# Who issues the second half of the first token tile: SyncE's queue or ScalarE

## The chip, the cores and the metric

The kernel runs on one core of one Trainium2 chip. The time is device microseconds of that core, the median of several runs. A profile is a single execution of the program, recorded by the hardware profiler; its span goes from the first to the last instruction of the core.

## The reference

The computation is a gated mix of two branches over one sequence `x` of 2048 tokens with 448 channels, all in float32:

```
g = sigmoid((x * gate_w).sum(-1))
q, k, v = split(x @ wqkv)                        # 16 heads of 28
a = (softmax over 8 keys, 2 tokens apart) @ wo   # sliding, dilated attention
b = relu(x @ w1 + b1)**2 @ w2 + b2               # 1792 hidden units
out = g * a + (1 - g) * b
```

## The kernel before

TensorE (PE in the profile) does all the large products. To keep nearly float32 accuracy, each operand is split into a high part (rounded to the matmul's type) and a low part (the rest), and each product is three matmuls: high by high, high by low, low by high. ScalarE (ACT) rounds to the high part, VectorE (DVE) subtracts it from the raw data to get the low part. GpSimd (POOL) does the products of the attention, which is too narrow for TensorE.

The tokens are cut into four chunks of 512; the 448 channels, over which the products sum, into three row tiles of 128 channels (k = 0, 1, 2) and one of 64 (k = 3), which is stored twice so that two 64-row matmuls can run side by side. The phases follow each other on TensorE: q, k and v of the chunks, then both layers of the MLP, with the output projection of the attention fitted in between. The order of all work is written out by hand; a counter of estimated TensorE time decides while the program is built where a piece of another engine's work is put.

The change is in the start. L629 to L634 clear a tile `zero` on VectorE and run 13 filler matmuls (`WARM`) on TensorE that need no input. From L637 on the first inputs are fetched: `raws[0]` (`wqraw` in the profile), the weights of q, and `rx` (`xraw`), the tokens of chunk 0 with channels on the partitions. The loop over k issues the weights of row tile k (L641, for k = 3 L644) and then its tokens (L646). For k = 0 the tokens come in two transfers of 256 tokens each (128 KB), for the others in one (256 KB). Behind them, on the same queue, come the weights of k and v (L651, L654) and the tokens of chunk 1 (L565). All of these are issued by SyncE (SP), one after another; 224 transfers of the program go that way, and no other engine issues any.

The splits follow at L656: for each k ScalarE rounds the weights (L657) and the two halves of the tokens (L664), except the very first half, which VectorE rounds (L662). ScalarE's first instruction is a table load that belongs to the first of these (L657). VectorE makes the low parts (L665, L667).

TensorE's first real matmuls are those of `qkv_first` (L255). It works on four blocks of 128 tokens, and for each k it does the pair of blocks 0 and 1 and then 2 and 3, six matmuls each: twice high by high, twice the weights' low part, twice the tokens' low part. The first six of a k need its weights and the first half of its tokens, the other six the second half as well. The thirteenth is the first of k = 1. Then come the matmuls with 64 rows (L186) for k = 3 and all later products.

A transfer that reuses a completion semaphore first waits for the earlier transfer on it. There are eight of these in turn, so from the ninth transfer on SyncE waits, before it issues, for an earlier one to have landed.

Of the kernel before, what the change touches and what calls it, by code (L numbers as in the profile page):

```python
# [22 lines left out]
CH = 512  # L23
# [34 lines left out]
def gated_mix_kernel(ctx: ExitStack, tc: tile.TileContext, xT, wqkv, w1, w2, wo, b1, b2, out):  # L58
    nc = tc.nc
# [437 lines left out]
    def raw_tile(name):  # L497
        return rawp.tile([P, 4, 512], F32, tag="raw", name=name)
# [139 lines left out]
    rx = raw_tile("xraw0")  # L638
    for k in range(4):
        if k < 3:  # L640
            nc.sync.dma_start(raws[0][:, k, :NQ], wqkv[0, :, k])  # L641
        else:
            for b, rows in ((0, slice(0, 64)), (1, slice(64, P))):
                nc.sync.dma_start(raws[0][rows, k, :NQ], wqkv[b, rows, k])  # L644
        for cols in ((slice(0, 256), slice(256, CH)) if k == 0 else (slice(0, CH),)):
            nc.sync.dma_start(rx[:, k, cols], xT[0, :, k, cols])  # L646

    for b, tag in ((1, "k"), (2, "v")):
        raw = attp.tile([P, 3, D], F32, tag=tag, name=f"wqraw{b}")
# [571 lines left out]
```

## Time and profile before

| | |
|---|---|
| Time, median of 3 runs | 413.23 us (413.23 to 413.26) |
| The profiled execution's own time | 413.8 us |
| Its span | 412.0 us |
| Granted TensorE clock, mean | 1.000 |
| DMA, whole span | 73.83 MB, mean 179 GB/s |
| Idle of ScalarE up to 12 us, by DMA of tokens | 2.8 us in 3 waits, longest 1.6 |
| Idle of ScalarE up to 12 us, by DMA of weights | 1.6 us in 2 waits, longest 1.4 |

A row of the timeline has the start and the duration in us, the engine, the line, the operation, what it writes and reads, the shapes and a count, and in brackets the idle time of the engine before it with what ended it. Neighbouring instructions that are alike stand in one row, so a duration can be that of several. `PEld` is TensorE's weight loader, which works ahead of the matmuls. `SPq` rows are the time that SyncE takes to issue a transfer, not the transfer itself. A table by stretch of time has, for each engine, the busy time and the count of instructions, and last the clock, the busy share of the 16 DMA engines and what they moved.

### The profile page before, as it was taken

How to read it: one execution, taken by the hardware profiler on the slowest of the kernel's cores; microseconds unless marked ns; L12 is line 12 of the kernel's file. 1: busy time of each engine (PE TensorE's matmuls, PEld its weight loads, DVE VectorE, ACT ScalarE, POOL GpSimd, SP SyncE). 2: the span in 40 equal slices, each digit the busy share in tenths (PEclk: the TensorE clock that was granted, in tenths of full speed). 3: DMA queues.
4: the chain of work that ended last, by engine and by line, in shares of the span. 5: the costliest groups of instructions: out<-in, count | busy, mean ns of one | idle time of the engine just before them, and what ended most of it. 6: DMA issues, size and time to landing. Idle time of an engine off the chain costs nothing.

```text
span 412.0 us, 9331 instructions
## 1 busy us (share of the span) xinstructions
PE 407.8 (99%) x3835; PEld 366.0 (89%) x3835; DVE 270.6 (66%) x430; ACT 210.4 (51%) x461; POOL 268.4 (65%) x167
## 2 busy tenths in 40 slices
PE   8999999999999999999999999999999999999997
PEld 7999999999888888888888888989898888888996
DVE  4590745276767766787656798879576677892354
ACT  4641646387775555444565535444653254346540
POOL 0000001955999999989989899999899977940000
PEclk9999999999999999999999999999999999999999
DMA  7999999979262315654112649765146530168304
GB/s 213 368 351 309 286 390 288 355 223 315 91 241 99 128 51 209 208 186 152 41 47 105 222 158 270 196 146 154 28 157 200 217 130 2 45 179 132 95 0 181
DMA packets 66763, 73.83 MB, mean 179 GB/s; under 512 B 33120, under 2 KB 59296, under 8 KB 66464
## 3 DMA queue, kind: packets, MB, share of 16 engines
q1 hardware_dynamic: 66720, 73.23, 55.4%
q8 instruction: 30, 0.49, 0.5%
q14 instruction: 13, 0.11, 0.1%
HBM read 45.74 MB, written 28.28 MB: 180 GB/s over the span
## 4 chain that ended last, share of the span: by engine, by line
PE 99%; DVE 0%; issue 0%
PE b L186 33%; PE h L186 32%; PE qkv L186 23%; PE a L186 7%; PE qkv L255 2%; PE warm L634 1%; PE a L993 1%; PE last L993 0%; DVE bt L872 0%; PE last L985 0%; PE a L985 0%; DVE zero L631 0%; DVE b1z L632 0%
## 5 line engine op out<-in xcount | busy, mean ns | idle before, releaser
L335 POOL TENSOR_TENSOR qk<-q,k 128x896 f32<-128x896 f32 x64 | 135.2, 2144 | 84.2 <-DMA k<-k_d 76.0
L342 POOL TENSOR_TENSOR av<-lg,v 128x896 f32<-128x896 f32 x64 | 119.2, 1957 | 6.2 <-DVE lg L336 5.6
L621 DVE TENSOR_TENSOR h<-h,h 128x512 fp32r<-128x512 f32 x56 | 38.4, 688 | 66.8 <-ACT h L624 66.5
L186 PE MATMUL qkv<-wqh,x 64*128 64x448 f32 x528 | 78.2, 359 | 0.0
L336 DVE TENSOR_REDUCE lg<-qk 128x32 f32<-128x896 f32 x64 | 67.0, 1074 | 0.0
L350 DVE TENSOR_REDUCE o<-av 128x112 f32<-128x896 f32 x64 | 66.4, 1070 | 0.1
L186 PE MATMUL b<-w2ah,h 64*128 64x448 f32 x448 | 66.3, 359 | 0.0
L186 PE MATMUL b<-w2bh,h 64*128 64x448 f32 x448 | 66.1, 359 | 0.0
L622 ACT ACTIVATE h<-h,b1z 128x512 f32<-128x512 f32 x56 | 36.7, 655 | 43.6 <-PE h L186 43.6
L186 PEld LDWEIGHTS qkv<-wqh,x 64*128 64x128 f32 x528 | 49.4, 184 | 3.6
L186 PE MATMUL qkv<-wql,x 64*128 64x448 f32 x264 | 47.7, 358 | 0.0
L186 PEld LDWEIGHTS b<-w2bh,h 64*128 64x128 f32 x448 | 42.1, 184 | 3.5
L186 PEld LDWEIGHTS b<-w2ah,h 64*128 64x128 f32 x448 | 42.0, 184 | 3.7
L205 ACT ACTIVATE st<-qkv 128x448 f32<-128x448 f32 x48 | 23.5, 542 | 34.3 <-PE qkv L186 31.7
L186 PE MATMUL b<-w2bl,h 64*128 64x448 f32 x224 | 40.7, 358 | 0.0
L186 PE MATMUL b<-w2al,h 64*128 64x448 f32 x224 | 40.5, 358 | 0.0
L623 ACT ACTIVATE h<-h 128x512 fp32r<-128x512 f32 x56 | 33.5, 598 | 1.7
L624 ACT ACTIVATE h<-h 128x512 f32<-128x512 f32 x56 | 33.3, 594 | 0.0
L573 ACT ACTIVATE h<-h 128x4 fp32r<-128x4 f32 (+1 forms) x35 | 7.2, 207 | 44.4 <-PE b L186 44.2
L186 PE MATMUL h<-x2b,w1h 64*128 64x512 f32 x168 | 28.1, 386 | 0.0
L186 PE MATMUL h<-x,w1h 64*128 64x512 f32 x168 | 28.1, 386 | 0.0
L186 PE MATMUL h<-x1b,w1h 64*128 64x512 f32 x168 | 28.1, 386 | 0.0
(150 smaller groups left out, 688.6 us busy)
## 6 DMA issues: line engine op xcount, KB each, us to landing
k<-k_d SPq DMA_DIRECT2D x8, 840.0 KB, 5.6
v<-v_d SPq DMA_DIRECT2D x8, 840.0 KB, 5.0
x_d<-x SPq DMA_DIRECT2D x11, 512.0 KB, 6.8
q_d<-st SPq DMA_DIRECT2D x8, 448.0 KB, 5.5
k_d<-st SPq DMA_DIRECT2D x8, 448.0 KB, 5.2
v_d<-st SPq DMA_DIRECT2D x8, 448.0 KB, 5.8
w1raw<-w SPq DMA_DIRECT2D x4, 896.0 KB, 9.2
q<-q_d SPq DMA_DIRECT2D x8, 448.0 KB, 3.6
```

The lines of the kernel that those rows point to most:

```text
L186: nc.tensor.matmul(acc.pt[:, :acc.n], a[rows], w[rows], start=acc.todo == acc.all, stop=acc.todo == 1)
L205: nc.scalar.activation(st[:, :, t % 2], pt[:, :D].rearrange("p (g c) -> p g c", g=G), AF.Copy)
L255: nc.tensor.matmul(acc.pt[:, :D], a, w, start=k == j == 0, stop=False)
L335: nc.gpsimd.tensor_mul(pr, q[:, s:s + 1].to_broadcast([P, W, C]), k[:, s:s + W])
L336: pending.append(lambda: nc.vector.tensor_reduce(lg[:, s], pr.rearrange("p w (h d) -> p w h d", h=HG), axis=AX.X, op=ALU.add))
L342: nc.gpsimd.tensor_mul(pr.rearrange("p (h d) w -> p w h d", h=HG), lg[:, s][:, :, :, None].to_broadcast([P, W, HG, DH]), v[:, s:s + W].rea ...
L350: nc.vector.tensor_reduce(o[:, g * C:(g + 1) * C], pr, axis=AX.X, op=ALU.add)
L573: nc.scalar.activation(ap, f32(ap), AF.Copy)
L621: nc.vector.tensor_sub(hl, pt, f32(hh))
L622: ops += [lambda pt=pt, r=r: nc.scalar.activation(pt, pt, AF.Relu, bias=b1t[:, f + r:f + r + 1]), lambda pt=pt, hh=hh: nc.scalar.activatio ...
L623: lambda pt=pt, hh=hh: nc.scalar.activation(hh, pt, AF.Square),
L624: lambda pt=pt, r=r, low=low: (nc.scalar.activation(pt, pt, AF.Square), at(delays[r], low))]
```

## The change

The tokens 256 to 511 of row tile k = 0 are issued by ScalarE's queue (`nc.scalar`) instead of SyncE's, and in the program's order before the first half. In the order of ScalarE's instructions the issue is the first one, ahead of the table load of L657 and the first weight split. On SyncE's queue one transfer is missing; the others keep their order. What is moved, where to, and all computation stay the same. From here on the profile of the changed kernel has line numbers that are up to 3 higher.

```diff
-        for cols in ((slice(0, 256), slice(256, CH)) if k == 0 else (slice(0, CH),)):
-            nc.sync.dma_start(rx[:, k, cols], xT[0, :, k, cols])
+        if k == 0:
+            nc.scalar.dma_start(rx[:, 0, 256:CH], xT[0, :, 0, 256:CH])
+            nc.sync.dma_start(rx[:, 0, 0:256], xT[0, :, 0, 0:256])
+        else:
+            nc.sync.dma_start(rx[:, k], xT[0, :, k])
```

The completion semaphores are dealt out in the program's order: the first and the second half of these tokens swap theirs, so the tokens of k = 3, issued later by SyncE, wait for the landing of ScalarE's transfer before they are issued, where before they waited for the first half.

## The prediction

> **What bounds the kernel now.** I read the page first: its span, its busy times and the chain of work that ended last.
>
> ```profile
> span 412.0 us, 9331 instructions
> PE 407.8 (99%) x3835; PEld 366.0 (89%) x3835; DVE 270.6 (66%) x430; ACT 210.4 (51%) x461; POOL 268.4 (65%) x167
> ...
> PE 99%; DVE 0%; issue 0%
> ```
>
> TensorE (PE) is busy for 407.8 of 412.0 us and the chain is PE for 99%. So the change can pay only where PE stands still or runs slowly, and everything behind such a place moves by what is won or lost there. The waits of the weight loader (PEld) over the whole span say where PE stands still (total, times, longest):
>
> ```profile
> PEld warm L634 <- DVE b1z L632: 1.2, 1, 1.2
> PEld a L993 <- issue: 0.3, 1, 0.3
> PEld qkv L186 <- ACT wqh L115: 0.3, 1, 0.3
> PEld qkv L255 <- ACT x L664: 0.3, 1, 0.3
> PEld qkv L255 <- ACT wqh L657: 0.2, 1, 0.2
> ```
>
> Only the last two concern the loads that the change touches. The 1.2 is the start, before the filler matmuls of L634. The two of 0.3 at L993 and L186 stand where matmuls change between 64 and 128 rows; the L993 one waits for nothing the profile shows, so I count neither as data. The timeline of the loader then dates the two that matter:
>
> ```profile
> 4.19 0.50 PEld L255 LDWEIGHTS qkv<-wqh,x 128*128 128x128 f32 x2 [0.15 <-ACT wqh L657]
> 4.74 0.70 PEld L255 LDWEIGHTS qkv<-wql,x 128*128 128x128 f32 x2
> 5.48 1.45 PEld L255 LDWEIGHTS qkv<-wqh,x 128*128 128x128 f32 x4
> 6.98 0.50 PEld L255 LDWEIGHTS qkv<-wql,x 128*128 128x128 f32 x2
> 7.49 0.39 PEld L255 LDWEIGHTS qkv<-wqh,x 128*128 128x128 f32 x2
> 8.13 0.30 PEld L255 LDWEIGHTS qkv<-wqh,x 128*128 128x128 f32 x2 [0.25 <-ACT x L664]
> ```
>
> The first real matmul comes at 4.19 after 0.15 us of idling, and the thirteenth (row tile k = 1) at 8.13 after 0.25. The pitch also changes: four loads from 5.48 to 6.98 are 0.375 us each. Later, on the PE timeline, four matmuls from 9.05 to 9.84 are 0.20 each:
>
> ```profile
> 1.19 3.14 PE L634 MATMUL warm<-zero 128*128 128x256 f32 x13 [1.19 <-DVE b1z L632]
> ...
> 9.05 0.96 PE L255 MATMUL qkv<-wqh,x 128*128 128x448 f32 x4
> 9.84 0.56 PE L255 MATMUL qkv<-wql,x 128*128 128x448 f32 x2
> ```
>
> PE thus runs at about half rate from 1.19 until about 7.0, 5.8 us. In that stretch a lost microsecond costs 0.20/0.375 = 0.53 us of later work. What releases the two waits stands on ScalarE's (ACT) timeline:
>
> ```profile
> 0.74 1.28 ACT L657 ACT_TABLE_LOAD   x1 [0.74 <-PEq L1213]
> 3.45 0.58 ACT L657 ACTIVATE wqh<-wqraw 128x448 fp32r<-128x448 f32 x1 [1.43 <-DMA wqraw<-wqkv]
> 5.62 0.42 ACT L664 ACTIVATE x<-xraw 128x256 fp32r<-128x256 f32 x1 [1.59 <-DMA xraw<-xT]
> 6.24 0.58 ACT L657 ACTIVATE wqh<-wqraw 128x448 fp32r<-128x448 f32 x1 [0.20 <-DMA wqraw<-wqkv]
> 7.66 0.72 ACT L664 ACTIVATE x<-xraw 128x256 fp32r<-128x256 f32 x2 [0.84 <-DMA xraw<-xT]
> 8.29 0.56 ACT L657 ACTIVATE wqh<-wqraw 128x448 fp32r<-128x448 f32 x1
> 9.26 0.72 ACT L664 ACTIVATE x<-xraw 128x256 fp32r<-128x256 f32 x2 [0.41 <-DMA xraw<-xT]
> ```
>
> So the weights of k = 0 are there at 3.45, the second half of the tokens of k = 0 (the transfer that moves) at 5.62, the tokens of k = 1 at 7.66. SyncE's queue issues them one after another:
>
> ```profile
> 0.75 0.39 SPq L641 DMA_DIRECT2D wqraw<-wqkv  x1
> 1.19 0.89 SPq L646 DMA_DIRECT2D xraw<-xT  x2
> 2.13 0.43 SPq L641 DMA_DIRECT2D wqraw<-wqkv  x1
> 2.60 0.43 SPq L646 DMA_DIRECT2D xraw<-xT  x1
> ...
> 5.26 0.58 SPq L646 DMA_DIRECT2D xraw<-xT  x1
> ```
>
> **The change part by part.** *Removed from SP:* one issue. Two take from 1.19 to 2.13, so one is 0.47 us, and every later issue of this queue can come 0.47 earlier until it has a landing to wait for. One wait changes hands: the tokens of k = 3, issued at 5.26 and so at 4.79 in future, wait for ACT's transfer instead of SP's first token half; it should be in by about 4, and only later weights stand behind that issue.
>
> *Added to ACT:* one issue ahead of the table load. The trace has no ACT issue. From 0 to the two issues of SP in 0.94 as bounds, I take 0.43, SP's own. ACT idles 1.43 us between the table load and 3.45, so this is covered; without that cover it would delay the first weight split by the same 0.43. Queued behind it are the table load and that split, for which PE waits.
>
> *Moved data, against k = 0.* The moved 128 KB (131 kB) now start beside the first weights instead of behind the first half of the tokens. The DMA view in three stretches (the last columns are clock, DMA share, GB/s):
>
> ```profile
> 1.50:3.00 1.50, 1.50 (x8) 1.50 (x8) 0.00 (x0) 0.52 (x1) 0.00 (x0) 1.00 0.75 209
> 3.00:4.00 1.00, 1.00 (x7) 1.00 (x5) 0.21 (x1) 0.55 (x1) 0.00 (x0) 1.00 0.55 129
> 4.00:7.60 3.60, 3.60 (x12) 3.12 (x12) 2.07 (x5) 1.02 (x3) 0.00 (x0) 1.00 0.96 271
> ```
>
> If all of it goes ahead of the weights at 209 GB/s, they land 0.63 later; if the free quarter of the engines takes it, 0 later. Earlier isn't possible, as nothing ahead of them goes away. I take 0.3, the middle. PE's first real matmul moves from 4.19 to 4.5 and costs 0.3 x 0.53 = 0.16 (bounds 0 to 0.33). This does not add to the end as long as PE then waits at 8.13 anyway: without that wait PE would have been ready at 8.13 - 0.25 = 7.88, now at 8.04.
>
> *Moved data, for k = 1.* Between 3 and 4 us the engines moved only 129 GB/s, after that 271. 131 kB taken out of the full stretch are 131/271 = 0.48 us, the same as the 0.47 of the issue. So the tokens of k = 1 land at 7.66 - 0.47 = 7.19. Bounds: 0, if the order of bytes is all that counts; 1.0, if the hole also fills up to 271 (142 kB more, 0.52 us). The weights of k = 1 come at 5.77 instead of 6.24 and their split ends near 6.3, so it isn't in the way. The token split of 0.42 ends at 7.61, PE could start near 7.66.
>
> *The sum.* The thirteenth matmul goes at the later of PE (8.04; 7.88 to 8.22) and data (7.66; 7.1 to 8.13). In this execution that gains 8.13 - 8.04 = 0.09, at most 0.25, at worst it loses 0.09. But the PE side rests on the half rate until 7.0 in this one execution. Where full rate comes sooner, PE is ready sooner, the wait at 8.13 is longer, and the whole 0.47 of the data is won. I take 0.25 between 0.09 and 0.47. Behind it nothing is late: twelve matmuls at 0.20 are 2.4, so k = 2 is wanted at 10.3, and its first token half is split by 9.26 + 0.42 = 9.7, before its own landing also moves forward. For the profiled execution that is its 413.8 us (span 412.0 and 1.8 around it) - 0.25 = 413.55; the runs have a median of 413.23, 0.57 below it, and the same step gives 413.0.
>
> A rule speaks against more than that. The Trainium skill, "DMA: Bandwidth & Descriptors", section "Issuing engines are not separate DMA queues", says that transfers issued by several engines share the same 16 DMA engines and interleave, so that only issue time is saved. By it the gain is the 0.47 of issue at most, with the first weights slowed from their first packet; the 129 GB/s between 3 and 4 us say that here the engines weren't full.
>
> **The rivals.** *The data comes much earlier.* Once the tokens of k = 0 come early, the next thing that ACT does is bound by the weights of k = 1: split to 6.3, token split 0.42, PE at 6.8 to 7.3 if the tokens of k = 1 land by 6.3 to 6.8. From 8.13 that gains 0.84 to 1.3, a time of 411.9 to 412.4. For it: the DMA hole. Against it: the tokens would have to land 0.9 sooner, near the upper bound, and PE to be at full rate by about 5.5.
>
> *It doesn't do what it says.* The DMA engines run at a share of 0.96 from 4 us on; if the bytes in order set the landing, k = 1 comes at 7.66 as before and the wait at 8.13 stays, with a later start hidden in it: 413.1 to 413.4.
>
> *Slower: the half rate lasts longer.* PE came to full rate 5.8 us after its work began, with a gap of only 0.15 at 4.19. The change can widen this gap to 0.15 + 0.3 to 0.63, since the thirteen filler matmuls stay as many. If a gap of that size makes the count start anew, full rate comes 5.8 us after 4.6, at 10.4 instead of 7.0: 3.4 us at half rate, 3.4 x 0.47 = 1.6 us lost, less the 0.25 of the wait that it swallows: 414.6. It decides from the gap that the clock no longer counts as busy; against it, PE would still be busy for (5.8 - 0.78)/5.8 = 87% of that stretch at the least.
> The Trainium skill, "TensorE: Matmul & The Clock Gate", Part 1, gives such a gate, which opens after a busy window of about 3.4 us that runs freely against the kernel. By it a missed window costs 3.4 x 0.47 = 1.6 us (an estimate from that page's figure and the rows), and the moment of full rate differs between executions; the 5.8 us here agree with one window missed.
>
> **How the numbers follow.** Forecast 0.45, much earlier data 0.18, nothing moves 0.22, half rate 0.15. The forecast is 413.0, its own range 412.7 to 413.35. I call 0.2%, 0.83 us, what a measurement can tell from no change, so faster means below 412.40 and slower above 414.06. The forecast and "nothing moves" are both within: 0.67. Faster is the second case, 0.18; slower the last, 0.15. The range leaves out the last case and the low end of the second (0.05): from 412.2, and to 413.7, which takes in a first weight 0.63 late with an ACT issue of 0.94.
>
> **What would show it.** In the changed profile: the table load at about 1.2; the first ScalarE split between 3.45 and 4.1 (right at 3.75); the second token half split directly behind it, without the wait of 1.59; SP's second weight issue at about 1.66; the token split of k = 1 near 7.2; PEld's wait of 0.25 at 8.13 gone or under 0.1. I am wrong if that split stays at 7.66, if the first one moves beyond 4.1, or if the pitch of 0.375 lasts beyond 8 us.

## The result, and the profile after

The changed kernel is slower: 415.30 us (median of 13 runs, 413.70 to 415.92) against 413.26 us (13 runs, 412.60 to 413.63), 2.04 us more by the medians; the ratio, which goes by the means (415.08 and 413.25), is 1.0042 with a 95% interval of 1.0030 to 1.0054. The forecast was 413.0, the range ended at 413.7. The runs of the changed kernel also spread over 2.2 us, those of before over 1.0. They fall into two groups: three from 413.70 to 413.96 (mean 413.83) and ten from 414.80 to 415.92 (mean 415.45), 1.6 us apart.

The page of the changed kernel (an execution of the upper group, 415.83) has the span, the busy times and the chain:

```profile
span 414.0 us, 9331 instructions
PE 408.4 (99%) x3835; PEld 376.8 (91%) x3835; DVE 270.4 (65%) x430; ACT 210.5 (51%) x461; POOL 268.5 (65%) x167
...
PE 98%; DMA 1%; DVE 0%; SPq 0%; issue 0%
```

The span is 2.0 us longer, and for the first time a transfer is in the chain that ended last. The waits of the weight loader over the whole span (total, times, longest) name it:

```profile
PEld qkv L255 <- ACT x L667: 1.7, 1, 1.7
PEld warm L634 <- DVE b1z L632: 1.2, 1, 1.2
PEld qkv L186 <- issue: 0.3, 1, 0.3
PEld a L996 <- issue: 0.3, 1, 0.3
```

The wait of 0.25 at 8.13 is gone, as forecast. The one of 0.15 before the first real matmul, which the forecast let grow by 0.3, is now 1.7. The loader's timeline dates it:

```profile
1.19 2.85 PEld L634 LDWEIGHTS warm<-zero 128*128 128x128 f32 x13 [1.19 <-DVE b1z L632]
5.76 0.50 PEld L255 LDWEIGHTS qkv<-wqh,x 128*128 128x128 f32 x2 [1.72 <-ACT x L667]
6.30 0.70 PEld L255 LDWEIGHTS qkv<-wql,x 128*128 128x128 f32 x2
7.05 1.45 PEld L255 LDWEIGHTS qkv<-wqh,x 128*128 128x128 f32 x4
8.54 0.70 PEld L255 LDWEIGHTS qkv<-wql,x 128*128 128x128 f32 x2
9.29 1.15 PEld L255 LDWEIGHTS qkv<-wqh,x 128*128 128x128 f32 x4
10.45 0.39 PEld L255 LDWEIGHTS qkv<-wql,x 128*128 128x128 f32 x2
```

The first real matmul goes at 5.76 instead of 4.19. The pitch is 0.375 until past 9.29 (four loads from 7.05 to 8.54 are 0.37 each, two from 10.45 on take 0.2 each), where before it changed near 7.0. So PE both starts late and stays at half rate 3 us longer. The name in brackets is the releaser that came last by the profile, ScalarE's token split; VectorE's timeline shows that the first token half was later still:

```profile
5.35 0.29 DVE L665 CAST x<-xraw 128x256 fp32r<-128x256 f32 x1 [4.21 <-DMA xraw<-xT]
```

That split began at 3.79 in the kernel before:

```profile
3.79 0.29 DVE L662 CAST x<-xraw 128x256 fp32r<-128x256 f32 x1 [2.65 <-DMA xraw<-xT]
```

ScalarE's own timeline in the changed kernel:

```profile
0.74 0.41 ACTq L646 DMA_DIRECT2D xraw<-xT  x1
1.18 1.28 ACT L660 ACT_TABLE_LOAD   x1 [1.18 <-PEq L1216]
4.26 0.58 ACT L660 ACTIVATE wqh<-wqraw 128x448 fp32r<-128x448 f32 x1 [1.79 <-DMA wqraw<-wqkv]
4.74 0.40 ACT L667 ACTIVATE x<-xraw 128x256 fp32r<-128x256 f32 x1
5.95 0.58 ACT L660 ACTIVATE wqh<-wqraw 128x448 fp32r<-128x448 f32 x1 [0.81 <-DMA wqraw<-wqkv]
7.54 0.72 ACT L667 ACTIVATE x<-xraw 128x256 fp32r<-128x256 f32 x2 [1.01 <-DMA xraw<-xT]
```

The issue takes 0.41 and the table load still ends long before the weights are there. The weights of k = 0 come at 4.26 (3.45 before), the moved half directly behind them (5.62 before), the tokens of k = 1 at 7.54 (7.66). All that was won is on what PE doesn't want first. The three stretches of the DMA view (share and GB/s last) show why:

```profile
1.50:3.00 1.50, 1.50 (x8) 1.50 (x8) 0.00 (x0) 0.97 (x1) 0.00 (x0) 1.00 0.66 165
3.00:4.00 1.00, 1.00 (x7) 1.00 (x5) 0.00 (x0) 0.00 (x0) 0.00 (x0) 1.00 1.10 259
4.00:7.60 3.60, 2.15 (x7) 1.71 (x7) 2.03 (x5) 1.52 (x4) 0.00 (x0) 1.00 0.87 283
```

The hole between 3 and 4 us is filled (259 GB/s for 129), but the first 1.5 us got slower (165 for 209), and in them the moved half takes its share from the weights: by the packet records of the traces, 127 of the weights' 128 rows had moved by 3.0 us in the kernel before, and 86 of them, with 65 rows of the moved half, in the changed one.

The two spans can be set against each other at the first matmul of L186, which follows the same 36 matmuls in both, first before and then after:

```profile
13.14 0.19 PEld L186 LDWEIGHTS qkv<-w7h,x 64*128 64x128 f32 x2 [0.30 <-ACT wqh L115]
```

```profile
15.15 0.19 PEld L186 LDWEIGHTS qkv<-w7h,x 64*128 64x128 f32 x2 [0.31 <-issue]
```

It is 2.01 later, so the whole loss is made by then. By the prices of the prediction: 1.57 us later at half rate is 1.57 x 0.53 = 0.84, less the 0.25 of the wait that it swallows, 0.59; another 3.0 us at half rate are 3.0 x 0.47 = 1.4; together 2.0. The two groups of runs fit these two prices: by the means the lower one lies 0.58 above the kernel before, the upper one another 1.6. That the half rate is what parts the groups is not shown for this kernel, of which only one execution was profiled. The experiments test whether these are two separate causes.

### The profile page after: what moved, and what is told of

It reads as the page before. It is cut to its first block, busy times and chain, and to the rows that moved or that the text cites. A ratio compares the mean times of both kernels' runs of the same rounds, so it can differ in the third digit from the quotient of the medians.

```text
span 414.0 us, 9331 instructions
## 1 busy us (share of the span) xinstructions
PE 408.4 (99%) x3835; PEld 376.8 (91%) x3835; DVE 270.4 (65%) x430; ACT 210.5 (51%) x461; POOL 268.5 (65%) x167
## 4 chain that ended last, share of the span: by engine, by line
PE 98%; DMA 1%; DVE 0%; SPq 0%; issue 0%
PE b L186 32%; PE h L186 32%; PE qkv L186 23%; PE a L186 7%; PE qkv L255 2%; DMA xraw<-xT 1%; PE a L996 1%; PE last L996 0%; DVE bt L875 0%; SPq L641 0%; PE last L988 0%; PE a L988 0%; DVE x L665 0%
## 5 line engine op out<-in xcount | busy, mean ns | idle before, releaser
L186 PE MATMUL qkv<-wqh,x 64*128 64x448 f32 x528 | 78.0, 358 | 0.0
L186 PE MATMUL b<-w2ah,h 64*128 64x448 f32 x448 | 67.2, 359 | 0.0
L186 PE MATMUL b<-w2bh,h 64*128 64x448 f32 x448 | 67.0, 359 | 0.0
L186 PEld LDWEIGHTS qkv<-wqh,x 64*128 64x128 f32 x528 | 50.2, 184 | 3.0
L186 PE MATMUL qkv<-wql,x 64*128 64x448 f32 x264 | 48.4, 359 | 0.0
L186 PEld LDWEIGHTS b<-w2bh,h 64*128 64x128 f32 x448 | 43.6, 184 | 2.1
L186 PEld LDWEIGHTS b<-w2ah,h 64*128 64x128 f32 x448 | 43.4, 184 | 2.2
L186 PE MATMUL b<-w2bl,h 64*128 64x448 f32 x224 | 41.4, 358 | 0.0
L186 PE MATMUL b<-w2al,h 64*128 64x448 f32 x224 | 41.3, 358 | 0.0
L186 PE MATMUL h<-x,w1h 64*128 64x512 f32 x168 | 28.5, 386 | 0.0
L186 PE MATMUL h<-x0b,w1h 64*128 64x512 f32 x168 | 28.5, 386 | 0.0
L186 PE MATMUL h<-x1b,w1h 64*128 64x512 f32 x168 | 28.5, 386 | 0.0
```

The source lines that it names most:

```text
L186: nc.tensor.matmul(acc.pt[:, :acc.n], a[rows], w[rows], start=acc.todo == acc.all, stop=acc.todo == 1)
```

## The experiments

The theories are named in the expectations: A, the gap in PE's work makes the half rate last longer; B, late data alone; A1, the place of a transfer in the stream sets what is late; C, a second issuing queue costs by itself.

**Filling the gap.** The changed kernel with more filler matmuls.

```diff
-WARM = 13
+WARM = 20
```

> The changed kernel with 20 filler matmuls instead of 13, so that PE is busy until about 5.4 us and the gap of 1.7 us before the first real matmul at 5.76 is filled. Theory A (most of the loss is the half rate lasting longer, because of the gap): 413.3 to 413.9 us, median near 413.5, runs close together; the pitch changes from 0.375 to 0.20 before 8 us; what is left over 413.26 (0.1 to 0.6) is the late first token half. Theory B (all of the loss is that the first matmul starts 1.57 us late): 414.8 to 415.5 as the changed kernel, since the filler brings no data.

414.19 us (11 runs, 413.75 to 416.47) against 413.23; ratio 1.0028 (1.0018 to 1.0039). The loader's timeline:

```profile
1.19 4.34 PEld L634 LDWEIGHTS warm<-zero 128*128 128x128 f32 x20 [1.19 <-DVE b1z L632]
6.24 0.30 PEld L255 LDWEIGHTS qkv<-wqh,x 128*128 128x128 f32 x2 [0.71 <-issue]
...
7.05 0.77 PEld L255 LDWEIGHTS qkv<-wqh,x 128*128 128x128 f32 x4
```

In this execution the data came later still (6.24), yet the first real matmuls already run at 0.2 each (four in 0.78). Some 1.1 of the 2.04 us are gone with no byte moved. The 0.96 that stays is more than theory A gave (0.1 to 0.6), and could be the late half or the fillers themselves. So the same fillers went into the kernel before:

> The kernel before with 20 fillers, as the control for the changed kernel with 20 fillers (414.19 us beside 413.23): the fillers are the same, only the transfers differ. If the 0.96 us that the fillers left there is the late first token half: this kernel stays near 413.4 to 413.8 us (its fillers end near 5.5 at half rate, sooner where full rate comes during them). If the 0.96 is the fillers' own length: 414.1 us or more.

413.96 us (11 runs, 413.53 to 414.12) against 413.55; ratio 1.0007 (0.9998 to 1.0017), between the two expectations. The 20 fillers cost some 0.4 by the medians, with an interval that includes none; between the two kernels with 20 fillers 0.96 - 0.41 = 0.55 us are left for the late data. This control is not a clean one: in the profile of this kernel the fillers push the first real matmul from 4.19 to 5.07, while in the changed kernel they end before the data is there (a gap of 0.71) and delay nothing. So the late data costs between 0.55 and 0.96, which takes in the 0.59 above, and the rest of the 2.04, 1.1 to 1.5, is the gap.

**The gap alone.** The kernel before, with its transfers untouched and fewer fillers.

```diff
-WARM = 13
+WARM = 6
```

> The kernel before with 6 filler matmuls instead of 13: transfers untouched, but PE idle for about 1.7 us between 2.5 and 4.19. Theory A (the gap lengthens the half rate): the first real matmul still at 4.2, 413.5 to 415.0 us, median near 414.2, runs spread over about 1.5 us, pitch 0.375 until 7.6 to 11. Theory B (only late data cost): 413.26, as before.

414.45 us (8 runs, 413.67 to 415.43) against 413.23; ratio 1.0029 (1.0019 to 1.0039).

```profile
4.10 0.50 PEld L255 LDWEIGHTS qkv<-wqh,x 128*128 128x128 f32 x2 [1.55 <-ACT wqh L657]
```

The first real matmul comes no later than in the kernel before (4.10), and by the medians the kernel with a gap of 1.55 us ahead of it is 1.22 us slower with no data late. Theory B falls. The profile itself doesn't show that cost: it is of the fastest of the 8 runs (413.67), and there full rate came at 7.21, as in the kernel before (7.20; these moments stand in the traces' clock records, on which the last section has more). That the half rate lasted longer in the other runs is inferred. More fillers than 13, on the other hand, bring the kernel before nothing:

> The kernel before with 16 fillers instead of 13. Theory A (13 fillers leave no gap that the half rate depends on, so more only push the first real matmul from 4.19 to about 4.6 where PE is at half rate): 413.2 to 413.6 us, no wider spread than before. If PE's gap of 0.15 already mattered: 412.8 to 413.1 us.

413.62 against 413.37 us; ratio 1.0004 (0.9995 to 1.0013), not told apart from no change.

**The order without ScalarE.** The kernel before, all on SyncE, only the halves swapped.

```diff
-        for cols in ((slice(0, 256), slice(256, CH)) if k == 0 else (slice(0, CH),)):
+        for cols in ((slice(256, CH), slice(0, 256)) if k == 0 else (slice(0, CH),)):
```

> The kernel before, all transfers on SyncE's queue, with only the two halves of the first tokens swapped: weights, second half, first half. Theory A1 (the first half is late because it is the third transfer in the stream): weights near 3.45, first half near 5.5, first real matmul near 5.9, 414.8 to 415.8 us, so the changed kernel's loss without ScalarE. Theory C (the second queue costs): first half near 4.3, 413.3 to 413.8 us.

416.19 us (6 runs, 414.61 to 416.32) against 413.60, more than the 415.8 that was expected at the most; ratio 1.0052 (1.0033 to 1.0072). VectorE's first split and the loader's first load:

```profile
6.03 0.29 DVE L662 CAST x<-xraw 128x256 fp32r<-128x256 f32 x1 [4.89 <-DMA xraw<-xT]
...
6.43 0.50 PEld L255 LDWEIGHTS qkv<-wqh,x 128*128 128x128 f32 x2 [2.40 <-issue]
```

The first half came later still than expected (6.03 for 5.5). Without any second queue the loss is there in full. It needs only that the first token half is the third transfer of the stream.

**The halves the other way round on the two queues.**

```diff
-            nc.scalar.dma_start(rx[:, 0, 256:CH], xT[0, :, 0, 256:CH])
-            nc.sync.dma_start(rx[:, 0, 0:256], xT[0, :, 0, 0:256])
+            nc.scalar.dma_start(rx[:, 0, 0:256], xT[0, :, 0, 0:256])
+            nc.sync.dma_start(rx[:, 0, 256:CH], xT[0, :, 0, 256:CH])
```

> The changed kernel with the two halves swapped: ScalarE issues tokens 0 to 255 first, SyncE tokens 256 to 511 behind the first weights. Theory A1 (place in the stream of bytes sets the landing): first half and weights land near 4.2 to 4.4, the second half near 5.3; first real matmul near 4.9, a gap of about 0.8, 413.3 to 414.8 us. Theory C' (the contention with the first weights is what costs): weights at 4.26 as in the changed kernel and the same 415.3 us.

413.81 us (11 runs, 413.35 to 415.71) against 413.23; ratio 1.0021 (1.0010 to 1.0032).

```profile
4.17 0.58 ACT L660 ACTIVATE wqh<-wqraw 128x448 fp32r<-128x448 f32 x1 [1.70 <-DMA wqraw<-wqkv]
...
4.36 0.29 DVE L665 CAST x<-xraw 128x256 fp32r<-128x256 f32 x1 [3.22 <-DMA xraw<-xT]
...
4.79 0.50 PEld L255 LDWEIGHTS qkv<-wqh,x 128*128 128x128 f32 x2 [0.75 <-ACT wqh L660]
```

The weights are as late as in the changed kernel (4.17 and 4.26), but the half that ScalarE issues is there with them, and most of the loss is gone. So the sharing with the weights costs about 0.7 us of landing, and the rest of the changed kernel's late start is the first half in third place. With 17 fillers in this order:

> The kernel in which ScalarE issues the first half, with 17 fillers instead of 13, which covers its gap of 0.75 us. Theory A (the spread of 413.35 to 415.71 is the half rate lasting longer): runs between 413.0 and 413.7, median 413.3, spread under 0.8. Theory B (late data alone): median 413.8 with the same spread.

413.97 us (12 runs, 413.29 to 414.65) against 413.60; ratio 1.0007 (0.9997 to 1.0018). The spread falls from 2.4 to 1.4 us, but not under 0.8, and the median stays 0.4 above the kernel before; the expected 413.3 was not reached. (The spread says little here: one of the 23 runs of the kernel before beside it took 415.43.) The profile, of the slowest of the twelve runs (414.65), has no gap ahead of the first real matmul and the full pitch from 6.01 on, and then a wait for the tokens of k = 1, which came at 8.49 (7.66 in the kernel before):

```profile
8.96 0.30 PEld L255 LDWEIGHTS qkv<-wqh,x 128*128 128x128 f32 x2 [1.36 <-ACT x L667]
```

So in that execution late data behind k = 0 cost the time, and not the half rate.

**A quarter of the bytes.** ScalarE issues the last 64 tokens only, SyncE the other 448 in two transfers.

```diff
-            nc.scalar.dma_start(rx[:, 0, 256:CH], xT[0, :, 0, 256:CH])
+            nc.scalar.dma_start(rx[:, 0, 448:CH], xT[0, :, 0, 448:CH])
             nc.sync.dma_start(rx[:, 0, 0:256], xT[0, :, 0, 0:256])
+            nc.sync.dma_start(rx[:, 0, 256:448], xT[0, :, 0, 256:448])
```

> The changed kernel with ScalarE issuing only the last 64 tokens (32 KB instead of 128 KB), SyncE tokens 0 to 255 and then 256 to 447. Theory A1 (cost by bytes ahead): weights near 3.65, first half near 4.2, first real matmul near 4.6, 413.3 to 414.2 us. Theory C (any transfer on the second queue costs the whole): first half beyond 5, 415 us.

414.96 us (12 runs, 413.38 to 415.76) against 413.60; ratio 1.0030 (1.0017 to 1.0042).

```profile
3.67 0.58 ACT L661 ACTIVATE wqh<-wqraw 128x448 fp32r<-128x448 f32 x1 [1.21 <-DMA wqraw<-wqkv]
...
4.59 0.29 DVE L666 CAST x<-xraw 128x256 fp32r<-128x256 f32 x1 [3.45 <-DMA xraw<-xT]
...
5.00 0.50 PEld L255 LDWEIGHTS qkv<-wqh,x 128*128 128x128 f32 x2 [0.96 <-ACT wqh L661]
...
6.29 1.45 PEld L255 LDWEIGHTS qkv<-wqh,x 128*128 128x128 f32 x4
7.79 0.70 PEld L255 LDWEIGHTS qkv<-wql,x 128*128 128x128 f32 x2
```

The weights are late by 0.22 for 32 KB and by 0.81 for 128 KB, about in proportion to the bytes. The first half is late by 0.8, more than the 0.4 expected; why is open. The time misses the expectation: a gap of 0.96 brings two thirds of the loss (1.36 of 2.04). In this profile, of a run near the median, it too keeps PE at about half rate, until past 7.79 where that ended near 7.0 before. Two of the twelve runs, at 413.38 and 413.68, lost next to nothing, the other ten took 414.76 and more: the same two groups. The loss doesn't go with the bytes, but with the gap that they make.

**Issued later.** Two kernels put ScalarE's issue behind other work. First behind a one-element ACTIVATE that brings the table load forward:

```diff
         if k == 0:
+            nc.scalar.activation(b1z[0:1, 14:15], none, AF.Copy)
             nc.scalar.dma_start(rx[:, 0, 256:CH], xT[0, :, 0, 256:CH])
```

> The changed kernel with a one-element ACTIVATE ahead of ScalarE's issue, so that the table load comes first and the transfer is issued at about 2.2 us instead of 0.74. Theory A1 (the loss comes from the moved transfer going ahead of the first weights and the first token half): weights land near 3.45 and the first half near 3.8 as before, first real matmul near 4.2, 412.8 to 413.4 us. Theory C (a second issuing queue as such, or SyncE's second transfer, is slow): the first half still near 5.3, 414.5 to 415.5 us.

416.09 us (6 runs, 414.47 to 417.16) against 413.23, above both expectations; ratio 1.0066 (1.0048 to 1.0085). The issue was not held back to 2.2 us:

```profile
0.74 1.28 ACT L646 ACT_TABLE_LOAD   x1 [0.74 <-PEq L1217]
1.21 0.37 ACTq L647 DMA_DIRECT2D xraw<-xT  x1
...
3.38 0.58 ACT L661 ACTIVATE wqh<-wqraw 128x448 fp32r<-128x448 f32 x1 [1.15 <-DMA wqraw<-wqkv]
5.72 0.42 ACT L668 ACTIVATE x<-xraw 128x256 fp32r<-128x256 f32 x1 [1.76 <-DMA xraw<-xT]
...
5.91 0.29 DVE L666 CAST x<-xraw 128x256 fp32r<-128x256 f32 x1 [4.77 <-DMA xraw<-xT]
```

ScalarE's queue issues at 1.21, while the table load still runs, at the same moment at which SyncE issues the first half. The weights are as early as before (3.38), and now the two halves share and both land near 5.8. The time expected under A1 was built on an issue at 2.2 that didn't happen; the landings fit A1, as the weights escape and the first half doesn't. Then the issue behind the first weight split:

```diff
         nc.scalar.activation(wqh[:, k, :D], raws[0][:, k, :D], AF.Copy)
+        if k == 0:
+            nc.scalar.dma_start(rx[:, 0, 256:CH], xT[0, :, 0, 256:CH])
```

> The changed kernel with ScalarE's issue put behind its first weight split, so that the transfer starts at about 3.4 us, when the first weights have landed; SyncE's queue is one issue shorter as in the changed kernel. Theory A1 (what costs is the moved transfer running beside the first weights and the first token half): first half near 3.8, first real matmul near 4.2, no gap over 0.3, thirteenth matmul at 7.7 to 8.2, 412.8 to 413.5 us. Theory C (a second issuing queue costs by itself): first half beyond 5, 414.5 us or more.

419.29 us (5 runs, 419.00 to 421.20) against 413.60; ratio 1.0147 (1.0125 to 1.0168).

```profile
3.46 0.38 ACTq L661 DMA_DIRECT2D xraw<-xT  x1
...
3.76 0.29 DVE L666 CAST x<-xraw 128x256 fp32r<-128x256 f32 x1 [2.62 <-DMA xraw<-xT]
...
11.15 0.42 ACT L668 ACTIVATE x<-xraw 128x256 fp32r<-128x256 f32 x1 [7.12 <-DMA xraw<-xT]
...
4.17 0.50 PEld L255 LDWEIGHTS qkv<-wqh,x 128*128 128x128 f32 x2
...
11.62 0.50 PEld L255 LDWEIGHTS qkv<-wqh,x 128*128 128x128 f32 x2 [5.46 <-ACT x L668]
```

The profile is of the slowest of the five runs (421.20). The front of it is as expected: first half at 3.76, first real matmul at 4.17 with no gap, with the second queue in use. That speaks against C. But the moved half, issued at 3.46, lands only at 11.15, and the second pair of blocks waits 5.46 us for it. The expected 412.8 to 413.5 was wrong: I had taken this transfer to land in the 2 to 4 us of the others.

**A version that might win.** The wait of 0.25 at 8.13 invites splitting the tokens of k = 1 too, on SyncE.

```diff
-        for cols in ((slice(0, 256), slice(256, CH)) if k == 0 else (slice(0, CH),)):
+        for cols in ((slice(0, 256), slice(256, CH)) if k < 2 else (slice(0, CH),)):
```

> The kernel before with the tokens of k = 1 also in two transfers on SyncE's queue. If the wait of 0.25 us at 8.13 is still worth something: the first half of k = 1 lands 0.3 to 0.7 earlier than 7.64, the wait goes, 412.8 to 413.2 us beside about 413.3 for the kernel before. If the additional issue (0.47 us for all that comes behind it) eats it: 413.2 to 413.6 us.

413.43 against 413.37 us; ratio 1.0002 (0.9993 to 1.0011), no change that can be told. In its profile PE came to full rate before 6.2, and then waited 0.43 there for the second half of k = 0 and 0.18 at 9.88 for k = 2: with the wait at 8.13 gone, the next transfers are the limit.

## Why the prediction was wrong, point by point

- *What bounds the kernel, where the change can pay, and the two waits*: right. The wait of 0.25 went, the one of 0.15 grew to 1.7, and the whole difference is made before the first matmul of L186.
- *Removed from SP, added to ACT*: right. SyncE's second weight issue is at 1.66, ScalarE's issue takes 0.41, and the table load at 1.18 is hidden.
- *Moved data, against k = 0*: this is the step that failed, and in two ways. I priced the delay of the weights alone, 0.3 with an upper bound of 0.63; it was 0.81. The bound divided the bytes by 209 GB/s, a rate measured with one queue, and with two it was 165 in the same stretch: 131/165 = 0.79. (In all profiles this stretch has 165 to 181 GB/s where ScalarE issues at about 0.74, and 195 to 209 where it doesn't.) And I left out the other operand of the first matmul. The first token half had been second in the stream with 225 KB ahead of it, and became the third with 353 KB: 5.35 instead of 3.79. The halves swapped on SyncE alone show that this place by itself is enough. The first real matmul moved by 1.57 us, where the bound was 0.63.
- *Moved data, for k = 1*: the size was off. The tokens came 0.12 earlier (7.54), not 0.47; the weights of k = 1 0.29 instead of 0.47.
- *The sum* took "the later of PE and data" at the thirteenth matmul, and PE's side was the wrong one by the term above. It also held the moment of full rate fixed at 7.0. With a gap of 1.72 us it went to about 10, which the rival had priced (3.4 us at half rate, 414.6) and I had given 0.15. Its chance hung on the size of the gap, so the first mistake carried over into it. The two kernels with 20 fillers and the one with 6 show that a gap by itself costs time and that it is the larger part here, 1.1 to 1.5 of 2.04 us. A count that starts anew is not how it decides: 5.8 us after 5.76 would be 11.6, and full rate came at 10.05. It goes by windows of time, as the last section works out. Two of the prediction's own signs of being wrong came true: the first ScalarE split beyond 4.1, and the pitch of 0.375 beyond 8 us.
- *The data comes much earlier* and *it doesn't do what it says*: neither. The DMA hole did fill, with bytes that PE didn't want yet.

## What to carry to other kernels

A transfer moved to another queue joins the stream at a new place. Before pricing the issue time that it saves, list every operand that the first waiting instruction needs and where each of them then stands. An operand that was third and becomes first pushes the others back.

At a cold start on TensorE a gap can cost time even where no data is late: by the medians 1.22 us for the 1.55 of the kernel with 6 fillers. Filler matmuls sized to end just when the data arrives are only as good as that arrival, and whatever delays the data has to lengthen the filler as well. That is no sure gain: 20 fillers took 1.1 us off the changed kernel's loss, 17 took nothing that can be told off the kernel with the halves the other way round.

## What the runs showed of the hardware

**Full rate came at the end of a window of 3.41 us in which TensorE was busy enough, and went at the end of one in which it stood still.** In the kernel with the issue behind the split, PE waits from about 6.2 to 11.62. The table by stretches (the column before the DMA share is the granted clock):

```profile
7.30:10.60 3.30, 0.00 (x0) 0.00 (x0) 0.00 (x0) 0.00 (x0) 0.00 (x0) 1.00 1.07 286
10.70:17.40 6.70, 5.78 (x16) 5.13 (x17) 5.75 (x13) 4.96 (x12) 0.00 (x0) 0.50 0.63 221
17.50:24.00 6.50, 6.50 (x50) 5.81 (x50) 0.00 (x0) 2.46 (x7) 0.00 (x0) 1.00 0.49 164
```

The clock falls to 0.50 at about 10.6 and returns at about 17.5, 5.9 us after the work has. In the kernel with the one-element ACTIVATE the fillers still run at half rate when a gap of 2.28 us begins at 4.04, and the first matmuls behind it run at full pitch:

```profile
6.32 0.30 PEld L255 LDWEIGHTS qkv<-wqh,x 128*128 128x128 f32 x2 [2.28 <-ACT x L668]
...
7.12 0.78 PEld L255 LDWEIGHTS qkv<-wqh,x 128*128 128x128 f32 x4
```

This profiled execution was the fastest of that kernel's six (414.47). The clock record of its trace puts the start of full rate at 4.60, inside the gap. Each trace's record begins with its first full rate: at 7.20 in the kernel before, at 10.05 in the changed one. (So the column shows 1.00 ahead of it too, and the slow start doesn't count in the mean.) Between two changes the records have stretches of 3.41, 6.83, 402.77, 406.19 and 409.60 us, which are 1, 2, 118, 119 and 120 times 3.413. The Trainium skill, "TensorE: Matmul & The Clock Gate", Part 1, describes windows of about 3.4 us that run freely against the kernel. These records agree with it.

Cut into such windows, the traces say what a gap does. First the window of the changed kernel with its gap in it, then two of the kernel with the ACTIVATE (length, then PE's busy time):

```profile
3.22:6.64 3.42, 1.97 (x8) 1.65 (x7) 1.29 (x4) 1.46 (x3) 0.00 (x0) 1.00 0.89 255
```

```profile
1.18:4.60 3.42, 3.14 (x13) 2.85 (x13) 0.00 (x0) 1.62 (x3) 0.21 (x4) 1.00 0.70 156
4.60:8.01 3.41, 1.66 (x8) 1.43 (x9) 2.03 (x5) 0.99 (x2) 0.00 (x0) 1.00 0.99 307
```

The first, busy for 58%, did not bring full rate; the second, 92%, did; the third, 49%, did not take it away, and the one with no work at all (7.22 to 10.63 in the kernel with the issue behind the split) did. Over all 13 profiles the windows that brought full rate have PE busy for 86% or more, those that didn't for 80% or less (76% in the kernel before, up to 3.79); these shares are estimates, as the ends of matmuls are modelled. So by this the same gap costs a window, some 1.6 us, or nothing, by where the windows fall in that execution (3.41 x 0.47 = 1.6, with the price of the prediction). This fits the two groups of runs.

**A transfer on the second queue can land late when the first queue has much to move.** Issued at 3.46, 128 KB took 7.7 us to land. By the packet record of that trace its first row moved at 6.37, 2.9 us after the issue, and in these SyncE's queue moved 528 kB; its last row moved at 9.95. Of the bytes from 7.3 to 10.6 (286 GB/s, above) a tenth was its own. Issued at 0.74 or 1.21, with little ahead, such a transfer had its first row moving after 1.2 and 1.4 us. The Trainium skill, "DMA: Bandwidth & Descriptors", section "Queues, rings and completion order", has each DMA engine change between the queues packet by packet. The 2.9 us without a row don't look like that, and why is open.

**The sequencer issues a transfer while the table load runs** (1.21 against 0.74 to 2.02), so the table load in front didn't hold the issue back here.
